# A fused attention and expert kernel: the expert's up products by one level of Strassen's scheme, with the weight sums loaded again for every pair of token chunks

## The chip, the core and the metric

The kernel runs on one core of a Trainium2 chip. The metric is the time of one execution on the device, in microseconds (us). The engines are named as in the profile: PE (TensorE, matrix products), PEld (PE's weight loads, listed apart), DVE (VectorE), ACT (ScalarE), POOL (GpSimd), SP (SyncE, which here only issues DMAs). PE reads its operands from the on-chip memory SBUF and writes to PSUM, which has 8 banks; a 128x512 tile of 32-bit numbers fills one bank.

## What is computed

```python
scores = scale * np.matmul(q, k.transpose(0, 1, 3, 2)) + bias   # 8 batches, 8 heads, 576 positions
attn = softmax(scores);  x = np.matmul(attn, v)                 # reshaped to 4608 tokens x 512

def _moe_ref(x, w1, w2, w3, w_out):      # 4608x512; 512x1024 twice; 1024x1024; 1024x512
    a = x @ w1
    b = x @ w2
    h = a * b @ w3
    return (h @ w_out).astype(np.float32)
```

The bias is a small network of the positions' distance. The expert weights come as 64-bit floats and are turned into 32-bit ones on the chip.

## The kernel before

The kernel has three stages. First it makes the bias; then it runs the attention of 32 units (pairs of heads by batches), whose result `x_d` (not yet divided by the softmax's sums) and the reciprocal sums `r_d` go to DRAM; then comes the expert. While attention still runs, the expert's weights `w3` and `w_out` are brought in, and `fold` multiplies them into one matrix (`folded`, L611), so that the expert is `(a * b) @ folded`.

Every 32-bit operand of a product is split into a high part in the reduced format fp32r and the rest: `xh` and `xl`, `wh` and `wl`, `gh` and `gl`. A product is three matmuls, high by high, low by high, high by low. So each split costs an ACT (or POOL) copy and a DVE subtraction.

The weights are turned into 32 bits by `narrow` (L121 to L150). Its steps for 512 columns are: one DMA (`wi`), two ACT instructions (L126, L129), four DVE instructions (L132, L135, L141, L146), and two POOL instructions (L149, L150), of which the first still reads `wi`. Before, `split_w` does this 16 times (8 blocks of 128 of the 1024 hidden columns, by `w1` and `w2`), then splits; all split weights stay in SBUF for the whole expert stage: the first two blocks in the pool `w01` on SBUF's right end, the other six in `wpool`.

The expert stage goes over 9 chunks of 512 tokens, and in each over the 8 blocks `ft`: 72 steps. In a step, `up` makes `a` and `b` for one block (24 matmuls of 128x512, L652), ACT copies `a` out of PSUM (L657), DVE multiplies it with `b` in PSUM (L660), and ACT and DVE split the product `g` (L663, L666); `down` multiplies the split product of the step before with `folded` (12 matmuls, L677), adding up over the 8 blocks in four PSUM banks `o`. `load_x` and `split_x` bring in and split the next chunk's tokens.

The order of the work on each engine is written out by hand: every piece of work is put into a list with a due time (`put(plan, steps, *times)`), and `drive` issues the pieces sorted by that time. An engine then takes its instructions strictly in that order, so one that waits holds up all behind it. The times are only used for sorting. `t_f` is the due time of the first expert step, and `end` that of attention's last piece. DMAs on SP are placed by the scheduler.

## Time and profile before

| what | value |
|---|---|
| median of 3 runs | 1249.78 us (1249.32 to 1249.95) |
| span of the profiled execution | 1248.1 us |
| PE busy | 1210.0 us (97%) |
| DVE, ACT, POOL busy | 653.6, 603.1 and 379.7 us |
| first matmul of the unbroken expert stage (`up`) | at 654.41 us |
| last group of matmuls (`o`) | from 1238.91 us, for 5.45 us |

The profiled execution's own span is 1248.1 us from the first to the last instruction, 1.7 us under the median of the runs; a change of the span is taken over to the median as it is. A matmul's listed duration holds its way through the pipeline; what one matmul costs in a row of them is the distance between starts, or the time of a group by its count.

### The profile page before, as it was taken

The page shows a single profiled execution, that of the slowest core. Times are in us where ns is not written, and L with a number is a line of the kernel's source. Part 1 is how long each engine was busy: PE and PEld are TensorE (multiplying, and loading weights), DVE is VectorE, ACT ScalarE, POOL GpSimd, SP SyncE. Part 2 cuts the span into 40 slices and gives each one's busy share as a digit, 9 for nine tenths or more (in the row PEclk, how much of TensorE's full clock was granted, in tenths as well). Part 3 has the DMA queues.
Part 4 walks back from the last instruction along what each step waited for, and adds up shares of the span by engine and source line. Part 5 has one row for each costly group of instructions (what it writes and reads, how often), then busy time and mean ns, then how long its engine had stood idle before and what let it go on. Part 6 is the DMA issues. An engine that isn't in the chain of part 4 may idle for free.

```text
span 1248.1 us, 19110 instructions
## 1 busy us (share of the span) xinstructions
PE 1210.0 (97%) x7200; PEld 964.2 (77%) x7200; DVE 653.6 (52%) x1380; ACT 603.1 (48%) x1295; POOL 379.7 (30%) x256
## 2 busy tenths in 40 slices
PE   6789999999999999999999999999999999999998
PEld 1368887777777788887678888888888888888887
DVE  8957776777677767775797522222212231313111
ACT  3768887888788878888444221212121212121211
POOL 5026664666466655661444300000000000000000
PEclk9989999999999999999999999999999999999999
DMA  4874446444644564521543121211111120200000
GB/s 149 285 234 144 142 147 202 142 142 141 222 123 151 151 219 134 145 81 54 133 147 110 60 68 34 68 34 51 51 51 51 42 61 34 68 34 1 20 15 34
DMA packets 60220, 130.26 MB, mean 104 GB/s; under 512 B 8928, under 2 KB 17504, under 8 KB 60128
## 3 DMA queue, kind: packets, MB, share of 16 engines
q1 hardware_dynamic: 59696, 129.02, 33.1%
q8 instruction: 57, 0.93, 0.3%
q14 instruction: 35, 0.29, 0.1%
q10 hardware_dynamic: 432, 0.02, 0.0%
HBM read 99.10 MB, written 29.92 MB: 103 GB/s over the span
## 4 chain that ended last, share of the span: by engine, by line
PE 81%; DVE 10%; DMA 4%; ACT 3%; issue 2%; SPq 0%; ACTq 0%; POOL 0%; DVEq 0%; POOLq 0%
PE up L652 32%; PE o L677 16%; PE pst L391 13%; PE s L284 11%; PE pst L349 5%; DVE r L322 4%; DVE ts L292 3%; PE wacc L611 2%; DMA nb_d<-bev 2%; ACT pt L357 2%; PE bacc L511 1%; DVE zdve L497 1%; DVE px L355 1%; DVE r L323 0%; DMA wi<-in_moe_w_dram 0%
## 5 line engine op out<-in xcount | busy, mean ns | idle before, releaser
L292 DVE CUSTOM_DVE_ANT_0 ts<-s,nb 128x576 f32<-128x576 f32 x256 | 184.6, 748 | 134.7 <-ACT pt L357 73.7
L660 DVE TENSOR_TENSOR g<-up,a 128x512 f32<-128x512 f32 x72 | 49.7, 691 | 343.4 <-PE up L652 343.4
L652 PE MATMUL up<-xh,wl 128*128 128x512 f32 x576 | 225.1, 391 | 0.0
L652 PE MATMUL up<-xl,wh 128*128 128x512 f32 x576 | 225.1, 391 | 0.0
L652 PE MATMUL up<-xh,wh 128*128 128x512 f32 x576 | 225.1, 391 | 0.0
L315 ACT ACTIVATE pp<-ts,mx 128x576 f32<-128x576 f32 x256 | 196.6, 769 | 42.5 <-DVE mx L292 42.5
L284 PE MATMUL s<-K,Q 128*128 128x288 f32 (+2 forms) x672 | 205.6, 325 | 9.2 <-ACT bev L518 3.7
L284 PE MATMUL s<-kl,Q 128*128 128x288 f32 (+2 forms) x672 | 182.3, 295 | 0.0
L677 PE MATMUL o<-w3s,gh 128*128 128x512 f32 x576 | 177.7, 390 | 0.0
L657 ACT COPY a<-up 128x512 f32<-128x512 f32 x72 | 42.2, 587 | 259.6 <-PE up L652 259.6
L638 POOL TENSOR_SCALAR xh<-xr 128x512 fp32r<-128x512 f32 x36 | 23.2, 646 | 445.4 <-DVE xr L634 442.7
L349 PE MATMUL pst<-ident,pp 128*128 128x128 f32 x1024 | 152.4, 277 | 0.2 <-ACT pt L357 0.2
L284 PEld LDWEIGHTS s<-K,Q 128*128 128x128 f32 x672 | 128.0, 191 | 30.1 <-DVE mx L292 13.6
L357 ACT ACTIVATE pt<-pst 128x512 f32<-128x512 f32 x224 | 129.4, 593 | 29.1 <-PE pst L349 24.8
L391 PE MATMUL pst<-pt,rv 128*64 128x320 f32 (+1 forms) x1024 | 138.3, 412 | 1.4 <-DVE pt L355 1.4
L663 ACT ACTIVATE gh<-g 128x512 fp32r<-128x512 f32 x72 | 45.5, 633 | 178.3 <-DVE g L660 178.3
L349 PEld LDWEIGHTS pst<-ident,pp 128*128 128x128 f32 x1024 | 118.5, 141 | 15.7 <-DVE wi L146 11.8
L284 PEld LDWEIGHTS s<-kl,Q 128*128 128x128 f32 x672 | 129.0, 192 | 0.0
L652 PEld LDWEIGHTS up<-xh,wl 128*128 128x128 f32 x576 | 108.2, 188 | 23.4
L652 PEld LDWEIGHTS up<-xl,wh 128*128 128x128 f32 x576 | 108.2, 188 | 23.4
L652 PEld LDWEIGHTS up<-xh,wh 128*128 128x128 f32 x576 | 108.2, 188 | 23.4
L677 PEld LDWEIGHTS o<-w3s,gh 128*128 128x128 f32 x576 | 108.1, 188 | 22.9
(87 smaller groups left out, 1734.2 us busy)
## 6 DMA issues: line engine op xcount, KB each, us to landing
rk<-in_k_dram SPq DMA_DIRECT2D x32, 576.0 KB
rq<-in_q_dram SPq DMA_DIRECT2D x32, 576.0 KB
wi<-in_moe_w_dram SPq DMA_DIRECT2D x32, 512.0 KB
nb_d<-bev SPq DMA_DIRECT2D x36, 295.5 KB
rv<-in_v_dram SPq DMA_DIRECT2D x32, 320.0 KB
x_d<-x SPq DMA_DIRECT2D x32, 288.0 KB
xr<-x_d SPq DMA_DIRECT2D x36, 256.0 KB
rb<-r_d SPq DMA_DIRECT2D x72, 128.0 KB
```

The source lines that it names most:

```text
L284: nc.tensor.matmul(o, l, r, start=(m == 0), stop=(m == len(ops) - 1))
L292: nc.vector.tensor_tensor_reduce(out=halves(ts), in0=d.pop(("s", t))[:, :, :HS], in1=halves(NB[p, t]), op0=ALU.add, op1=ALU.min, scale=-1. ...
L315: nc.scalar.activation(pp, ts, AF.Exp, bias=mx, scale=-1.0, accum_out=d["sum"][:, col:col + 1])
L322: nc.vector.tensor_scalar(r, d["sum"], 1e-9, None, op0=ALU.add)
L349: nc.tensor.transpose(ps[:, c * P:(c + 1) * P], x, ident)
L357: nc.scalar.activation(o, x, AF.Copy)
L391: nc.tensor.matmul(acc[rows], x[:, c0:c0 + D], m, start=(c == 0), stop=(c == 4))
L652: nc.tensor.matmul(acc, l[:, cc], r, start=(n == 0), stop=(n == 3 * NC - 1))
L657: nc.scalar.copy(a, ps[0])
L660: nc.vector.tensor_tensor(g, ps[1], a, op=ALU.mult)
L663: nc.scalar.activation(gh, g, AF.Copy)
L677: nc.tensor.matmul(d["o", t], l[:, sl], folded[ft][:, r], start=(ft == 0 and n == 0), stop=(ft == NF - 1 and n == 2),)
```

## The change

The expert works on 6 pairs of chunks of 384 tokens (called c and d) instead of 9 chunks of 512. For one block, `[a_c a_d; b_c b_d]` is a 2x2 block product: weights `[w1; w2]` cut in two halves of the inner dimension, tokens cut by chunk and by the same halves. Strassen's scheme (in Winograd's form) makes it with 7 block products instead of 8, from 4 more sums of weight blocks and 4 more sums of token blocks. A block product has 2 inner slices by 3 split terms, 6 matmuls of 128x384, so a step (pair, block) has 42 of them, and 18 matmuls of 128x512 in `down` (9 for d, 9 for c). There are 48 steps.

- `prep_w` replaces `split_w`: it runs `narrow` on both matrices of a block side by side, makes the 4 sums (L579), splits 7 blocks of weights (L583, L586) into one tile `wS` and writes it to DRAM (`w_d`, 1.83 MB for a block). Blocks 0 to 2 are prepared before the first step, blocks 3 to 7 in steps 0 to 4. `load_w` loads a block's `wS` again for each of pairs 1 to 5, into three buffers.
- `split_x` does the same for tokens: two multiplications of 768 columns (L654), 4 differences of 384 (L657), 7 copies and 7 subtractions (L663, L665), for each of two inner slices, once per pair.
- The 7 products accumulate in two PSUM banks `X` and `Y`: products 1, 6, 7, 4 in X, product 2 and then 5, 3 (called Z) in Y. Partial sums are read out between the products: by ACT (`p`, `u`, `z`; L705) and by DVE (`ac`, `bd`, `ad`, and the two products `gc`, `gd`; all L701). Each bank has one buffer, so the next product into a bank waits for the read before it. The other six banks hold the output sums.
- The buffers of `narrow` for the two matrices (pools `cva` and `cv2`) have one buffer each; before, `cv2` had two.

```diff
-    CH = 512
+    CH = 384
+    W2 = 2 * CH
-    STEP = 7.8
+    STEP = 11.40
-    cv = moe.enter_context(tc.tile_pool(name="cv2", bufs=2, side="right"))
+    cv = prep.enter_context(tc.tile_pool(name="cv2", bufs=1, side="right"))
+    bg = prep.enter_context(tc.tile_pool(name="bg", bufs=2, side="right"))
+    def prep_w(t):
+        big = bg.tile([P, 8, 2 * P], F32, name="big")
...
+            runs.append(narrow((cva, cv)[m], src, NC * P, flat[:, m * NC * P:(m + 1) * NC * P], nc.sync, pieces=NC))
+        for steps in zip(*runs):
+            for step in steps:
+                step()
+                yield
+        for o, x, y, op in ((4, 2, 3, ALU.add), (6, 0, 2, ALU.subtract), (5, 4, 0, ALU.subtract), (7, 1, 5, ALU.subtract)):
+            nc.vector.tensor_tensor(big[:, o], big[:, x], big[:, y], op=op)
+        yield
+        w = wr.tile([P, 2, 7, 2 * P], F32R, name="wS")
+        for o, x, n in ((0, 0, 2), (2, 3, 2), (4, 5, 2), (6, 7, 1)):
+            nc.scalar.activation(w[:, 0, o:o + n], big[:, x:x + n], AF.Copy)
+            yield
+            eng = nc.vector if o < 4 else nc.gpsimd
+            eng.tensor_tensor(w[:, 1, o:o + n], big[:, x:x + n], f(w[:, 0, o:o + n]), op=ALU.subtract)
+        nc.sync.dma_start(w_d[t], f(w.rearrange("p h s n -> p (h s n)")))
+        ups[0, t] = w
+    def load_w(p, t):
+        w = wr.tile([P, 2, 7, 2 * P], F32R, name="wS")
+        nc.sync.dma_start(f(w.rearrange("p h s n -> p (h s n)")), w_d[t])
...
+    AT_P = {"2": 0.0, "1": 1.04, "6": 4.2, "5": 5.25, "7": 6.3, "3": 7.3, "4": 10.4}
+    AT_E = {
+        "p": 2.10, "ac": 2.70, "u": 5.28, "z": 6.35, "bd": 7.32, "ad": 8.36, "gd": 8.95, "hd": 9.60, "ld": 10.15,
+        "gc": 11.45, "hc": 12.05, "lc": 12.60,
+    }
+    AT_D = {"d": 2.1, "c": 8.3}
+        if n in ("p", "u", "z"):
+            st[n] = temp("puz".index(n), n)
+            nc.scalar.copy(st[n], st["Z" if n == "z" else "X"])
+        elif n == "ac":
+            add("ac", 4, st["Y"], st["p"], ALU.add)
+        elif n == "bd":
+            add("bd", 3, st["X"], st["z"], ALU.add)
+        elif n == "ad":
+            add("ad", 5, st["Z"], st["u"], ALU.add)
+        elif n == "gc":
+            add("gc", 6, st["X"], st["ac"], ALU.mult)
+        elif n == "gd":
+            add("gd", 7, st["ad"], st["bd"], ALU.mult)
...
+    wr = moe.enter_context(tc.tile_pool(name="wr", bufs=3))
+    xs = moe.enter_context(tc.tile_pool(name="xs", bufs=1))
+    ps_ab = moe.enter_context(tc.tile_pool(name="ps_ab", bufs=1, space=PSUM))
```

How the rows move (in the rows of now, the lines from L579 on are the changed kernel's). First PE, in a late step of the expert stage. Before, a step begins with one block's 12 matmuls into `up0` and 12 into `up1` (here the last six into `up1`), and then the 12 of `down` into four output banks:

```order
L652 MATMUL up1_12187<-xh2_11656,wh17_8818 128x512
L652 MATMUL up1_12187<-xh2_11656,wl17_8820 128x512
L652 MATMUL up1_12187<-xl2_11657,wh17_8818 128x512
L652 MATMUL up1_12187<-xh3_11707,wh17_8818 128x512
L652 MATMUL up1_12187<-xh3_11707,wl17_8820 128x512
L652 MATMUL up1_12187<-xl3_11708,wh17_8818 128x512
L677 MATMUL o0_11922<-w3s6_8270,gh_12170 128x512 x2
L677 MATMUL o0_11922<-w3s6_8270,gl_12172 128x512
```

Now, from the start of the last step, products 2 and 1, the first output bank of d's `down`, and then products 6, 5 and 7 (each product is one row for each of the two inner slices):

```order
L692 MATMUL Y_13106<-xS0_12005,wS_12939 128x384 x3
L692 MATMUL Y_13106<-xS1_12301,wS_12939 128x384 x3
L692 MATMUL X_13117<-xS0_12005,wS_12939 128x384 x3
L692 MATMUL X_13117<-xS1_12301,wS_12939 128x384 x3
L732 MATMUL od0_12590<-w3s6_8283,ghd_13096 128x512 x2
L732 MATMUL od0_12590<-w3s6_8283,gld_13098 128x512
...
L692 MATMUL X_13117<-xS0_12005,wS_12939 128x384 x3
L692 MATMUL X_13117<-xS1_12301,wS_12939 128x384 x3
L692 MATMUL Y_13145<-xS0_12005,wS_12939 128x384 x3
L692 MATMUL Y_13145<-xS1_12301,wS_12939 128x384 x3
L692 MATMUL X_13117<-xS0_12005,wS_12939 128x384 x3
```

The matmuls are shorter and no longer alternate between spare banks: X_13117 is filled, read out and filled further within the step, and Y_13145 takes the bank of Y_13106.

Second ACT, among the expert's first steps. Before, in the first chunk, the copies `a` and `gh` of a step stand between the pieces of two blocks of `split_w` (`wmag`, `w` and `wh` belong to it):

```order
L126 ACTIVATE wmag<-wi 128x512
L129 ACTIVATE w<-wi 128x512
L657 COPY a<-up_8489 128x512
L568 ACTIVATE wh_8545<-w 128x512
L663 ACTIVATE gh<-g 128x512
```

Now, in step 1 of the first pair, from the two L126 of block 4's `prep_w` to the copies `p`, `u` and `z` (L705) of that step; the L583 rows belong to block 3:

```order
L126 ACTIVATE wmag<-wi 128x512 x2
L583 ACTIVATE wS<-big 128x512
L129 ACTIVATE big<-wi 128x512
L718 ACTIVATE ghc<-wos_8458 128x384
L129 ACTIVATE big<-wi 128x512
L583 ACTIVATE wS<-big 128x512 x2
L705 COPY wos_8494<-X 128x384
L583 ACTIVATE wS<-big 128x256
L705 COPY wos_8522<-X 128x384
L705 COPY wos_8530<-Y 128x384
```

Seven instructions of weight preparation and one split now stand ahead of `p` (`wos_8494`), the first of them behind a DMA.

Third DVE, at the same place. Before, `g` and `gl` of a step stand between the pieces of `split_w` and `split_x`:

```order
L132 TENSOR_SCALAR wmag<-wmag 128x512
L135 TENSOR_SCALAR wmag<-wmag 128x512
L660 TENSOR_TENSOR g<-up_8512,a 128x512
L141 SCALAR_TENSOR_TENSOR wmag<-wi,wmag 128x512
L571 TENSOR_TENSOR wl_8550<-w,wh_8545 128x512
L666 TENSOR_TENSOR gl<-g,gh 128x512
L146 TENSOR_SCALAR wi<-wmag 128x512
```

Now, in step 1 of the first pair, from the second L132 of block 4 to the sums of its weights, `ac` (`wos_8497`) stands ahead of the second half of `narrow`, and `bd`, `ad`, `gd` and the split `gld` behind it:

```order
L132 TENSOR_SCALAR wmag<-wmag 128x512
L135 TENSOR_SCALAR wmag<-wmag 128x512
L586 TENSOR_TENSOR wS<-big,wS 128x512
L135 TENSOR_SCALAR wmag<-wmag 128x512
L701 TENSOR_TENSOR wos_8497<-Y,wos_8494 128x384
L141 SCALAR_TENSOR_TENSOR wmag<-wi,wmag 128x512 x2
L146 TENSOR_SCALAR wi<-wmag 128x512 x2
L701 TENSOR_TENSOR wos_8545<-X,wos_8530 128x384
L701 TENSOR_TENSOR wos_8561<-Y,wos_8522 128x384
L701 TENSOR_TENSOR wos_8563<-wos_8561,wos_8545 128x384
L721 TENSOR_TENSOR gld<-wos_8563,ghd 128x384
L579 TENSOR_TENSOR big<-big 128x256 x4
```

So the weight preparation of a later block now waits for `ac`, which waits for `p` on ACT.

More of the change, by code (lines that the diff above doesn't have):

```diff
@@ L677, in down, with store, at, until @@
                 nc.tensor.matmul(
-                    d["o", t], l[:, sl], folded[ft][:, r],
+                    d["o", j, t], l[:, sl], folded[ft][:, r],
                     start=(ft == 0 and n == 0), stop=(ft == NF - 1 and n == 2),
                 )
-        yield
-        if ft == NF - 1:
-            for t in range(NT):
-                o = op.tile([P, DO], F32, name="osb")
-                nc.scalar.copy(o, d["o", t])
-                nc.sync.dma_start(out[c * CH + t * P:c * CH + (t + 1) * P, :], o)
-                yield
+    def store(p, j, t):
+        o = op.tile([P, DO], F32, name="osb")
+        move("DVE" if t == 1 else "ACT", (o, pairs[p]["o", j, t]))
+        r0 = p * W2 + "cd".index(j) * CH + t * P
+        nc.sync.dma_start(out[r0:r0 + P, :], o)
+    def at(time, step, *args):
+        later.append((time, len(later), lambda: step(*args)))
+    def until(time):
+        nonlocal later
+        now, later = [e for e in later if e[0] <= time], [e for e in later if e[0] > time]
+        drive(now)
     for i in range(NF):
```

199 lines of the change are left out of this document (107 added, 92 removed).

## The prediction

> **What bounds the kernel now.** I read the page first, then the chain of work that ended last, then the stretches of time around the start of the expert stage, and then the rows of single instructions. The chain in order of time (start, length, what) shows the expert stage as PE alone:
>
> ```profile
> span 1248.1 us, 19110 instructions
> 608.96 5.88 DMA wi<-in_moe_w_dram
> 648.83 5.58 PE wacc L611 x24
> 654.41 10.07 PE up L652 x43
> 1184.32 5.61 PE up L652 x24
> 1225.32 5.44 PE up L652 x24
> 1233.47 5.44 PE up L652 x24
> 1238.91 5.45 PE o L677 x24
> ```
>
> From 654.41 to 1238.91 + 5.45 = 1244.36 are 589.95 us, and a step starts every 8.15 us. So a matmul of 512 columns costs 5.44 / 24 = 0.2267 us. In the first two steps of a chunk, whose weights lie in `w01` at SBUF's right end, it costs 5.61 / 24 = 0.234, and in `fold`, whose weights lie on the right too, 5.58 / 24 = 0.2325. I call these the quick and the slow pace.
>
> Ahead of it, the stretches (length, then busy us and count of PE, PEld, DVE, ACT, POOL; clock, DMA share, GB/s) show DVE next to PE:
>
> ```profile
> 602.00:612.00 10.00, 8.75 (x44) 7.27 (x45) 8.18 (x14) 4.81 (x9) 2.65 (x2) 1.00 1.06 274
> 612.00:622.00 10.00, 9.02 (x45) 7.12 (x45) 5.48 (x11) 5.04 (x9) 3.65 (x4) 1.00 0.37 104
> 622.00:632.00 10.00, 7.97 (x30) 6.10 (x29) 9.50 (x14) 2.41 (x4) 4.94 (x6) 0.83 0.63 195
> 632.00:642.00 10.00, 10.00 (x52) 8.18 (x51) 8.63 (x12) 4.53 (x9) 5.66 (x4) 1.00 0.42 129
> 642.00:654.00 12.00, 12.00 (x59) 9.81 (x58) 11.52 (x18) 6.89 (x12) 5.63 (x4) 1.00 0.37 125
> ```
>
> In these 52 us DVE is busy for 43.3, and PE lost 4.3 us of the first 30. Anything that puts more on DVE here delays the expert's start.
>
> **The matmuls.** 384 columns occur nowhere; the nearest are the attention's scores of 288 columns, whose weights lie on the right:
>
> ```profile
> 400.42 0.29 PE L284 MATMUL s<-kl,Q 128*128 128x288 f32 x1
> 401.20 0.29 PE L284 MATMUL s<-kl,Q 128*128 128x288 f32 x1
> L284 PEld LDWEIGHTS s<-kl,Q 128*128 128x128 f32 x672 | 129.0, 192 | 0.0
> ```
>
> Six starts apart make 0.78 / 6 = 0.130 us for 288 columns; the slow pace has 0.2325 for 512. Both are 0.00045 us a column, so the cost goes with the columns. For 384 that gives 0.75 x 0.2267 = 0.170 at the quick pace and 0.75 x 0.2325 = 0.174 at the slow one. The new weights lie left, where the pace was quick; the token blocks of the odd pairs lie right, and whether that slows PE no row shows. I take 0.171, with 0.170 and 0.174 as ends. A step then costs 42 x 0.171 + 18 x 0.2267 = 7.18 + 4.08 = 11.26 us, 48 steps 540.6 us: **49.4 us gained** (42 to 51).
>
> The Trainium skill has a formula for this ("TensorE: Matmul & The Clock Gate", section Back-to-back issue gap): columns by 2.4 GHz and 2.5 ns on top. It would give 0.2158 for 512 columns, where this trace has 0.2267, and 0.1625 for 384; as an estimate from that page the gain would be 45 us and the sum 4 us higher. The measured pace stands.
>
> **The new evictions.** These are the rows by line and form (count, busy us, mean ns of one, idle before):
>
> ```profile
> L657 ACT COPY a<-up 128x512 f32<-128x512 f32 x72 | 42.2, 587 | 259.6 <-PE up L652 259.6
> L660 DVE TENSOR_TENSOR g<-up,a 128x512 f32<-128x512 f32 x72 | 49.7, 691 | 343.4 <-PE up L652 343.4
> L663 ACT ACTIVATE gh<-g 128x512 fp32r<-128x512 f32 x72 | 45.5, 633 | 178.3 <-DVE g L660 178.3
> L634 DVE TENSOR_TENSOR xr<-xr,rb 128x512 f32<-128x512 f32 x36 | 26.7, 743 | 0.0
> L605 DVE TENSOR_TENSOR w3l<-w3t,w3h 128x512 fp32r<-128x512 f32 x16 | 10.9, 682 | 4.1 <-ACT w3h L603 4.1
> L126 ACT ACTIVATE wmag<-wi 128x512 f32<-128x512 f32 x40 | 26.7, 667 | 7.1 <-DMA wi<-in_moe_w_dram 6.8 <-DVE w3l L605 0.3
> L129 ACT ACTIVATE w<-wi 128x512 f32<-128x512 uint32 x16 | 10.7, 670 | 0.0
> L132 DVE TENSOR_SCALAR wmag<-wmag 128x512 f32<-128x512 f32 x40 | 22.7, 568 | 3.9 <-ACT wmag L126 3.9
> L135 DVE TENSOR_SCALAR wmag<-wmag 128x512 int32<-128x512 int32 x40 | 20.8, 521 | 1.1
> L141 DVE SCALAR_TENSOR_TENSOR wmag<-wi,wmag 128x512 int32<-128x512 int32 x40 | 28.3, 707 | 0.2
> L146 DVE TENSOR_SCALAR wi<-wmag 128x512 int32<-128x512 int32 x40 | 18.0, 450 | 0.9
> L149 POOL TENSOR_TENSOR w<-w,wi 128x512 f32<-128x512 f32 x16 | 21.5, 1344 | 40.0 <-issue 20.2 <-ACT w L129 9.4 <-ACT wmag L126 5.5
> L150 POOL TENSOR_TENSOR w<-wmag,w 128x512 f32<-128x512 f32 x16 | 23.2, 1448 | 1.3
> ```
>
> Scaled to 384 columns, a read of PSUM costs 0.44 on ACT and 0.52 on DVE, a split 0.475 and 0.56. In a step of pairs 1 to 5, DVE has 7 of them (3.7 us) and ACT 5 (2.3 us) under 11.26 us of PE; the token splits add at most 4.5 us to a step. That is hidden as work. The waits are the question. Product 7 waits for `u`, product 3 for `z`, and the next step's product 1 for `gc`; each time, one product (6 x 0.171 = 1.03 us) covers the handover. Its legs, in four rows:
>
> ```profile
> 899.70 0.39 PE L652 MATMUL up<-xh,wl 128*128 128x512 f32 x1
> 899.73 0.59 ACT L657 COPY a<-up 128x512 f32<-128x512 f32 x1 [4.07 <-PE up L652]
> 616.62 0.69 DVE L605 TENSOR_TENSOR w3l<-w3t,w3h 128x512 fp32r<-128x512 f32 x1 [0.64 <-ACT w3h L603]
> 617.37 0.65 PE L599 MATMUL w3t<-ident,w3s 128*128 128x128 f32 x4 [0.98 <-DVE w3l L605]
> ```
>
> ACT starts 0.03 us after the next product's first matmul, and PE starts 0.06 us after DVE's end (617.31). So a handover takes 0.03 + 0.52 + 0.06 = 0.61 at most and has 0.4 us to spare: I cost these waits at nothing. The reload of `wS`, 1.83 MB a step, takes 6.7 us at the 274 GB/s of the first stretch above, and may start when the step three before ends, two steps (22 us) ahead: nothing as well. On SP it stands behind the loads of the next pair's tokens, which wait for the one `xr` and `rb` buffer, and at a pair's start behind the output stores, which wait for `down`'s last sums; both are ready within the step in which they stand, so the queue can hold a reload up by one step at most, of the two that it has. If that cover went, product 2 would be late next, by what is missing of 6.7 us. The stores themselves are as before, three at the end instead of four; I leave their half us out.
>
> **The start.** Between DVE's first `w3s` (601.9) and the fold's last `w3l` the new order has 14 `w3l` and 7 `w3s` (21 x 0.682 = 14.3), six rounds of `narrow` (6 x 2.246 = 13.5), 4 multiplications of 768 (4 x 1.11 = 4.5), 22 token differences and splits (22 x 0.56 = 12.3), 8 weight sums of 256 (8 x 0.37 = 3.0) and 4 weight splits (2.7): 50.3 us. With the 8.7 us of idle that the same stretch has now, it takes 59 instead of 52: **7 us lost**; nothing if the idle closes, 15 if the idle doubles.
>
> **The first pair.** Blocks 3 to 7 are prepared in steps 0 to 4. Each matrix has one `wi` buffer, so the second matrix of a block can be fetched only when POOL has read the last one, and its fetch stands ahead of `p` on ACT. The loop from landing to landing, in the order of the instructions: on ACT the second L126, a weight split, L129, `ghc`, L129, two weight splits and `p` (0.667 + 0.633 + 0.67 + 0.475 + 0.67 + 1.27 + 0.44 = 4.83); on DVE `ac`, two L141, one L146 (0.52 + 1.41 + 0.45 = 2.38); on POOL L149, L150, L149 (4.14); then the fetch:
>
> ```profile
> 684.40 0.37 SPq L121 DMA_DIRECT2D wi<-in_moe_w_dram  x1
> 687.93 0.67 ACT L126 ACTIVATE wmag<-wi 128x512 f32<-128x512 f32 x1 [0.73 <-DMA wi<-in_moe_w_dram]
> 670.74 1.62 POOL L150 TENSOR_TENSOR w<-wmag,w 128x512 f32<-128x512 f32 x1
> 671.14 1.51 DVE L132 TENSOR_SCALAR wmag<-wmag 128x512 f32<-128x512 f32 x1
> ```
>
> It takes 3.5 us here, and 5.88 in the chain above beside other transfers; beside the 1.83 MB store of `w_d` I take 4.3. With eight handovers of 0.05 the loop is 16.0 us, 4.8 more than a step of PE. Four loops lie between the five blocks: 19 us. In step 0 `p` comes 4.8 us after the landing instead of at product 1's end (2.1): 2.7. In step 3 one multiplication enters the loop: 1.1. In step 4 `gc` stands behind the four sums and a token split, and product 1 waits for it: about 3. Together **26 us lost**. The low end is DVE's bare work, 11.0 us a step and 8 more for the token blocks of steps 3 and 4: 8 us. The high end has the 5.88 us fetch and one blocking of DVE a loop, such as L132's 1.51 above, which ended with POOL's L150, against 0.568 on average: 19 us a loop, so 38 us. POOL is no bound here: 4 narrow instructions and two weight splits are some 7 us of the 16. PE will idle for 5 us a step; in the stretch from 622 to 632, with 2 us of idle, the granted clock fell to 0.83, and if it does so here the products get longer where PE waits anyway, so I add nothing.
>
> The Trainium skill gives a rule for that blocking ("SBUF — State Buffer", section SBUF: two separate sides): DVE and GpSimd share a port pair under an exclusive lock, and the loser waits for the whole instruction. The trace agrees (1.51 us). If it struck in each loop, the sum would be some 5 us higher.
>
> **The sum.** 1249.78 - 49.4 + 7 + 26 = 1233.4 us. The sum is made in the profiled span, 1.7 us under the median, and carried over.
>
> **Rivals.**
> - *The bank handovers miss* (slower). If `u`, `z` and `gc` each come x us late, that is 3 x 48 x = 144 x: 0.13 us each over their slack cancels what the sum has left, 0.2 gives about 1262. For it: with one bank each, every product waits for a read. Against it: the slack of 0.4 us. Chance 0.12.
> - *Weight loads set the pace* (slower). A load lasts 0.192, more than 0.171. If loads went one behind the other, a step would be 42 x 0.192 + 4.08 = 12.14 us, the gain only 7 us, and the time 1276. Against it: the scores run at 0.130 with loads of 0.192. Chance 0.03.
> - *The first pair is hidden after all*: both losses at their low ends, 1249.8 - 49.4 + 2 + 10 = 1212. For it: a fetch of 3.5 us and POOL shorter than its listed spans. Chance 0.15.
> - *Gain and losses cancel*, at their high ends: about 1250. Chance 0.10.
> - My forecast, 1222 to 1246, has the remaining 0.60.
>
> The range from 1211 to 1256 leaves out some 2 in 10. A change of 0.2% (2.5 us) is about what this measurement can tell: faster 0.73, the same 0.10, slower 0.17.
>
> **What would show it.** Pairs 1 to 5: 11.2 to 11.4 us a step, PE without idle time; if idle time stands before L692 there, the first rival holds. Steps 0 to 4: about 16 us each, PE idle behind ACT's `p` and DVE's `gc`, ACT's L126 behind DMA `wi`. First product 2 some 7 us after 654. I am wrong if the steps of the later pairs are above 11.7 us, or if those of the first pair are not above 12.

## The result: the kernel is 0.6% slower

The changed kernel takes 1258.2 us (1256.9 to 1259.3 in four runs) against 1249.9 in the same comparison: a ratio of 1.0061, interval 1.0047 to 1.0076. The forecast was 1233.5. First the page of the changed kernel, its span and the busy times of the engines:

```profile
span 1256.4 us, 20346 instructions
PE 1185.7 (94%) x7488; PEld 998.4 (79%) x7488; DVE 796.5 (63%) x1700; ACT 669.3 (53%) x1479; POOL 378.9 (30%) x236
```

PE works 24 us less than before and yet the span is 8.3 us longer. The stretches of time say where PE stands idle (length, then busy us and count of PE, PEld, DVE, ACT, POOL; clock, DMA share, GB/s):

```profile
632.00:642.00 10.00, 7.20 (x35) 5.69 (x35) 6.70 (x14) 1.79 (x3) 5.08 (x4) 1.00 0.87 306
664.00:700.00 36.00, 27.08 (x121) 24.28 (x120) 25.57 (x49) 15.36 (x31) 16.32 (x13) 0.88 0.55 197
700.00:750.00 50.00, 38.10 (x170) 32.23 (x169) 44.43 (x71) 20.28 (x42) 25.74 (x18) 0.92 0.46 168
800.00:1200.00 400.00, 400.00 (x2086) 373.24 (x2086) 195.81 (x355) 118.12 (x246) 0.00 (x0) 1.00 0.57 205
```

From 800 to 1200 PE is never idle. Between 664 and 750 it lacks 20.8 us, DVE is the busiest engine beside it (44.4 of the last 50), and the granted clock is 0.88 and 0.92. The matmuls into bank Y show when steps begin. In step 0 product 1 was done ahead, inside the fold, so its rows into Y are products 2, 5 and 3; then come the first products 2 of step 1 (678.84), of steps 6 and 7, and of two late steps:

```profile
665.66 1.21 PE L692 MATMUL Y<-xS,wS 128*128 128x384 f32 x6
672.11 2.29 PE L692 MATMUL Y<-xS,wS 128*128 128x384 f32 x6 [3.00 <-DVE wos L701]
678.84 1.21 PE L692 MATMUL Y<-xS,wS 128*128 128x384 f32 x6
763.91 1.20 PE L692 MATMUL Y<-xS,wS 128*128 128x384 f32 x6
775.40 1.20 PE L692 MATMUL Y<-xS,wS 128*128 128x384 f32 x6
1224.21 1.22 PE L692 MATMUL Y<-xS,wS 128*128 128x384 f32 x6
1235.73 1.22 PE L692 MATMUL Y<-xS,wS 128*128 128x384 f32 x6
```

An undisturbed step takes 11.49 us where the tokens lie on the left (763.91 to 775.40) and 11.52 where they lie on the right. Steps 0 to 5 would take 6 x 11.49 less product 1 and less `down`, which step 0 has not: 63.7 us. They took 763.91 - 665.66 = 98.25, so the first pair lost 34.6 us.

Not all of that is idle time. PE stands idle for 22.6 of the 98.25 us; in the other 75.7 it does what takes 63.7 undisturbed. Most of that difference is the granted clock, which was 0.50 in four stretches, at about 671 to 677, 698 to 701, 729 to 735 and 753 to 756 us. Two pieces of them, and product 7 of step 0, which lies in the first:

```profile
672.00:677.00 5.00, 4.89 (x15) 4.89 (x16) 2.49 (x6) 0.48 (x1) 3.25 (x3) 0.50 0.90 356
730.00:735.00 5.00, 5.00 (x15) 4.50 (x16) 4.28 (x11) 3.79 (x8) 0.00 (x0) 0.50 0.51 127
674.20 2.12 PE L692 MATMUL X<-xS,wS 128*128 128x384 f32 x6
```

Product 5 took 674.20 - 672.11 = 2.09 us there, where an undisturbed product takes 1.04. By the distances between starts, the longer matmuls of the four stretches add up to 8.8 us; the last 3.2 go mostly to the ends and the first matmuls of PE's runs, at some twelve stops. Each of the four stretches came with or shortly after an idle time of PE of 2.4 to 5.0 us, while one of 2.5 us (before product 1 of step 1) brought none, so no limit is read from this.

The last group of attention's products shows when the expert's start could begin, in the chain of before and in that of after:

```profile
595.43 2.84 PE pst L391 x20
```

```profile
597.63 2.84 PE pst L391 x20
```

From its end to the first product 2 of the expert (before, the first `up`) are 654.41 - 598.27 = 56.1 us before and 665.66 - 600.47 = 65.2 now. I call this the start's distance. Attention itself ended 2.2 us later, though its work is unchanged. In the ten kernels below with the same attention this group starts at 595.9 to 599.0 (the last in e1, whose expert has no Strassen products), so I take the 2.2 us as the difference of one execution from another.

| part | forecast | measured |
|---|---|---|
| expert matmuls, undisturbed | -49.4 | -38.8 |
| start's distance | +7 | +9.1 |
| end of attention in this execution | - | +2.2 |
| first pair | +26 | +34.6 |
| from the last step to the end (by what is left) | -0.5, left out | +1.3 |
| sum | -16.4 | +8.4 (span: +8.3) |

The -38.8 is 763.91 to 1247.25 for steps 6 to 47, plus 63.7 and the last `down` of 4.1, against 589.95; 1.0 of it is product 1 of step 0, done ahead in the fold. So the forecast failed by two terms above all: the matmuls gained 10.6 us less, and the first pair lost 8.6 us more.

### The profile page after: what moved, and what is told of

Same layout as the page of the kernel before. It is cut to its first block, busy times and chain, and to the rows that moved or that the text cites. A ratio compares the mean times of both kernels' runs of the same rounds, so it can differ in the third digit from the quotient of the medians.

```text
span 1256.4 us, 20346 instructions
## 1 busy us (share of the span) xinstructions
PE 1185.7 (94%) x7488; PEld 998.4 (79%) x7488; DVE 796.5 (63%) x1700; ACT 669.3 (53%) x1479; POOL 378.9 (30%) x236
## 4 chain that ended last, share of the span: by engine, by line
PE 72%; DVE 15%; DMA 4%; ACT 4%; issue 2%; POOL 2%; SPq 0%; ACTq 0%; DVEq 0%; POOLq 0%
PE X L692 15%; PE pst L391 13%; PE Y L692 11%; PE s L284 11%; PE od L732 7%; PE oc L732 7%; PE pst L349 5%; DVE r L322 4%; DVE ts L292 3%; ACT pt L357 2%; DMA nb_d<-bev 1%; PE bacc L511 1%; DVE xS L665 1%; DVE zdve L497 1%; POOL big L149 1%
## 5 line engine op out<-in xcount | busy, mean ns | idle before, releaser
L292 DVE CUSTOM_DVE_ANT_0 ts<-s,nb 128x576 f32<-128x576 f32 x256 | 184.6, 748 | 135.4 <-ACT pt L357 74.1
L692 PE MATMUL X<-xS,wS 128*128 128x384 f32 x1152 | 237.4, 341 | 18.1 <-DVE wos L701 16.6
L692 PEld LDWEIGHTS X<-xS,wS 128*128 128x128 f32 x1152 | 207.3, 190 | 29.6 <-DVE wos L701 19.2
L692 PE MATMUL Y<-xS,wS 128*128 128x384 f32 x864 | 177.4, 340 | 4.5 <-DVE wos L701 4.5
L692 PEld LDWEIGHTS Y<-xS,wS 128*128 128x128 f32 x864 | 155.6, 191 | 5.9 <-DVE wos L701 5.8
L701 DVE TENSOR_TENSOR wos<-X,wos 128x384 f32<-128x384 f32 x96 | 53.4, 557 | 151.0 <-PE X L692 151.0
L349 PEld LDWEIGHTS pst<-ident,pp 128*128 128x128 f32 x1024 | 118.6, 141 | 15.7 <-DVE wi L146 11.8
L705 ACT COPY wos<-X 128x384 f32<-128x384 f32 x96 | 45.9, 478 | 137.7 <-PE X L692 137.6
L391 PEld LDWEIGHTS pst<-pt,rv 128*64 128x64 f32 x1024 | 67.8, 136 | 50.1 <-issue 10.4
L732 PE MATMUL od<-w3s,ghd 128*128 128x512 f32 x288 | 91.9, 401 | 0.0
L732 PE MATMUL oc<-w3s,ghc 128*128 128x512 f32 x288 | 89.6, 392 | 0.0
L701 DVE TENSOR_TENSOR wos<-Y,wos 128x384 f32<-128x384 f32 x96 | 53.4, 556 | 54.1 <-ACT wos L705 37.9
L251 POOL TENSOR_TENSOR Q<-rq,Q 64x1152 fp32r<-64x1152 f32 x32 | 85.4, 2669 | 2.7
```

The lines of the kernel that those rows point to most:

```text
L251: nc.gpsimd.tensor_tensor(Qd[hi], x[hi], f(Qd[hi]), op=ALU.subtract)
L292: nc.vector.tensor_tensor_reduce(out=halves(ts), in0=d.pop(("s", t))[:, :, :HS], in1=halves(NB[p, t]), op0=ALU.add, op1=ALU.min, scale=-1. ...
L349: nc.tensor.transpose(ps[:, c * P:(c + 1) * P], x, ident)
L391: nc.tensor.matmul(acc[rows], x[:, c0:c0 + D], m, start=(c == 0), stop=(c == 4))
L692: nc.tensor.matmul(acc, w[:, l, W_AT[n], i * P:(i + 1) * P], x[:, r, X_AT[n]], start=(k in "125" and i == 0 and m == 0), stop=(i == 1 and ...
L701: nc.vector.tensor_tensor(st[o], x, y, op=op)
```

## The experiments

A ratio is that of a kernel's times to those of before, run on the same chip; the changed kernel's own is 1.0061.

| kernel | median us | ratio (interval) | start's distance | first pair lost |
|---|---|---|---|---|
| changed kernel | 1258.2 | 1.0061 (1.0047 to 1.0076) | 65.2 | 34.6 |
| e3, no preparation of blocks 3 to 7 | 1225.1 | 0.978 (0.9758 to 0.9802) | 64.6 | 1.9 (8 steps) |
| e4, second raw-token buffer | 1257.3 | 1.0037 (1.002 to 1.0054) | 63.6 | 35.1 |
| e5, two `wi` buffers | 1271.4 | 1.0176 (1.0154 to 1.0198) | 64.9 | 30.5 |
| e6, preparation spread | 1246.3 | 0.9965 (0.995 to 0.9979) | 66.5 | 22.8 (8 steps) |
| e7, spread and later | 1252.8 | 1.0014 (1.0 to 1.0028) | 65.3 | 30.3 (8 steps) |
| e9, e7 with e4 | 1249.7 | 0.9999 (0.9983 to 1.0015) | 63.8 | 30.5 (8 steps) |
| e10, no token split in the first pair | 1254.0 | 1.0017 (1.0002 to 1.0033) | 64.7 | 31.6 |
| e11, blocks 4 to 7 converted in attention | 1236.7 | 0.988 (0.986 to 0.9901) | 63.8 | 13.0 |
| e12, all blocks | 1271.3 | 1.0161 (1.0137 to 1.0186) | 59.4 | 5.0 |
| e13, e12 with a new start | 1264.9 | 1.01 (1.0079 to 1.0121) | 51.5 | 6.1 |
| e14, e11 with a new start | 1233.9 | 0.9863 (0.9841 to 0.9884) | 61.9 | 12.0 |
| e15, e14 with blocks 3 to 6 | 1235.2 | 0.9873 (0.9849 to 0.9898) | 61.9 | 14.1 |
| e16, POOL's part of narrow on DVE | 1257.2 | 1.0044 (1.003 to 1.0059) | 64.5 | 33.9 |
| e17, e14 with that | 1234.0 | 0.986 (0.9844 to 0.9877) | 62.7 | 11.0 |

One correction to the expectations below: in those of e3 to e7 and e9 I took the row at 672.11 for the first product 2. It is product 5 of step 0; product 2 stands at 665.66. So "28 us" of the first pair there is 34.6, "6.5 us forward" in e7's text was no change at all, and the "8 us" that the second buffer is said to bring in those of e7 and e9 is 1.6. The waits of DVE for tokens that the texts of e4 and e14 give as 8.3, or 6 and 8 us, were 3.3, or 3.0 and 3.3 (see e4).

### What a matmul of 384 columns costs (e1, e2)

```diff
-    CH = 512
+    CH = 384        # e2: 256; both in the kernel before
```

> The kernel before, with chunks of 384 tokens instead of 512 (12 chunks, the same plain 24 up matmuls a step, no Strassen). It measures the pitch of a 384-column matmul by itself. Theory A (a matmul has a fixed cost: 512 columns cost 0.2267 us = 512 / 2.4 GHz + 13.4 ns, so 384 cost 0.160 + 0.0133 = 0.1733 us): 24 matmuls take 4.16 us in the steps with weights on the left. Theory B (the prediction's: the cost goes with the columns, and the 0.1733 to 0.1746 us of the changed kernel come from its own pattern, six matmuls into one bank and then a change of bank): 24 matmuls take 4.08 us here (0.170 each). For the first two blocks of a chunk, whose weights lie on SBUF's right end, A says 0.180 each (4.32 us), B 0.1755 (4.21 us).

> The kernel before, with chunks of 256 tokens (18 chunks): a third point for the pitch. Theory A (fixed cost of 13.4 ns a matmul): 0.1067 + 0.0134 = 0.120 us each, 24 in 2.88 us. Theory B (cost goes with the columns): 0.1133 us each, 2.72 us. If something else than PE sets the step here (evictions of 72 steps become 144), the pitch is read within a block of 12 matmuls.

The chain of e1 in the expert stage (start, length, what), and a row of e2's:

```profile
802.58 4.18 PE up L652 x24
808.84 4.16 PE up L652 x24
815.08 4.17 PE up L652 x24
```

```profile
785.14 2.87 PE up L652 x24
```

A matmul of 384 columns costs 4.18 / 24 = 0.1742 us and one of 256 costs 0.1196, beside 0.2267 for 512. Theory A holds for weights on the left, and the plain kernel without any Strassen products has the same price. Between 256 and 512 a column costs (0.2267 - 0.1196) / 256 = 0.418 ns; 256 columns at that price are 0.107, so 0.0126 us of every matmul do not depend on its columns. The steps at 808.84 and 815.08, whose weights lie on SBUF's right end, are not slower: the slow pace that both theories priced at 0.1755 to 0.18 did not show at 384 columns. (The kernels took 1267.6 and 1284.6 us in their one run, as shorter chunks need more matmuls.)

### The weight preparation (e3, e10)

```diff
-    for t in range(NF):              # e3: which blocks prep_w makes
+    for t in range(3):
-        w, n = ups[p, t], int(k)
+        w, n = ups[p, t % 3 if p == 0 else t], int(k)
```

> The changed kernel without the weight preparation of blocks 3 to 7: in the first pair their products use the weights of blocks 0 to 2, and the later pairs load those three again from DRAM (the same bytes). The number of matmuls, evictions, token splits and loads stays. Theory A (the preparation in steps 0 to 4 costs the first pair its 28 us): the first six steps take 11.5 us each but for the token splits, the loss falls from 28 to 2 to 6 us, and the kernel takes 1232 to 1237 us. Theory B (the handovers between the two banks or the token splits of the second pair, which stand in steps 3 to 7, hold the first pair): at least 15 of the 28 us stay, and the kernel takes 1245 us or more.

Product 2 of step 0 and of step 8 in e3:

```profile
665.65 1.22 PE L692 MATMUL Y<-xS,wS 128*128 128x384 f32 x6
754.24 1.21 PE L692 MATMUL Y<-xS,wS 128*128 128x384 f32 x6
```

Eight undisturbed steps are 86.7 us here; these took 88.6, and the granted clock stayed at 1.00. That is theory A; its time came out 7 us too high since it reckoned with 28 us instead of 34.6. So 32.7 of the 34.6 us come with the preparation of blocks 3 to 7, 6.5 us a block, and the span fell by just that, from 1256.4 to 1223.8. The bank handovers and the token splits by themselves cost the first pair 1.9 us at most. The start is where it was: block 3's preparation does not delay it.

```diff
     def split_x(p, i):               # e10
+        if p == 1:
+            ...
+            nc.sync.dma_start(f(x), f(pairs[0]["x"][i]))
+            return
```

> The changed kernel without the token split of the second pair, which stood in steps 3 to 7 of the first: the second pair uses a copy of the first pair's split tokens, brought by a DMA. The weight preparation stays as it is. The first pair lost 34.5 us against undisturbed steps (product 2 of step 0 at 665.66, step 6 at 763.91), and 1.9 without the preparation of blocks 3 to 7 but with the token split. Theory A (each costs its own: the weight loop of 16 us a block alone): at least 28 us stay lost, 1253 us or more. Theory B (the two meet on DVE, whose bare work of 82 us in the first pair nearly fills PE's 87, so the split costs 10 to 15 us where the preparation runs, though 2 alone): 20 to 25 us lost, 1245 to 1251 us.

It lost 31.6 us, as theory A said, though a little of that is its own: the copies slowed one fetch to 8.47 us. What it shows best is the loop. ACT's L126 of the second matrix of blocks 4 to 7 (start, length, idle time before it):

```profile
685.30 0.67 ACT L126 ACTIVATE wmag<-wi 128x512 f32<-128x512 f32 x1 [0.77 <-DMA wi<-in_moe_w_dram]
700.66 0.67 ACT L126 ACTIVATE wmag<-wi 128x512 f32<-128x512 f32 x1 [0.93 <-DMA wi<-in_moe_w_dram]
716.41 0.67 ACT L126 ACTIVATE wmag<-wi 128x512 f32<-128x512 f32 x1 [1.32 <-DMA wi<-in_moe_w_dram]
732.30 0.66 ACT L126 ACTIVATE wmag<-wi 128x512 f32<-128x512 f32 x1 [1.07 <-DMA wi<-in_moe_w_dram]
```

The distances are 15.4, 15.8 and 15.9 us; the forecast had 16.0. In the changed kernel itself, blocks 3 to 6:

```profile
668.66 0.65 ACT L126 ACTIVATE wmag<-wi 128x512 f32<-128x512 f32 x1
681.03 0.67 ACT L126 ACTIVATE wmag<-wi 128x512 f32<-128x512 f32 x1 [0.47 <-DMA wi<-in_moe_w_dram]
697.72 0.67 ACT L126 ACTIVATE wmag<-wi 128x512 f32<-128x512 f32 x1 [0.93 <-DMA wi<-in_moe_w_dram]
713.04 0.66 ACT L126 ACTIVATE wmag<-wi 128x512 f32<-128x512 f32 x1 [0.86 <-DMA wi<-in_moe_w_dram]
731.33 1.25 ACT L126 ACTIVATE wmag<-wi 128x512 f32<-128x512 f32 x2
```

Here they are 12.4, 16.7, 15.3 and 18.9 (the last row holds both matrices of block 7), and only the last, into which the token split of steps 3 and 4 falls, does not wait for the DMA.

### The loop, or the work in it? (e5, e6, e16)

```diff
-            wi = pool.tile([P, n, 2], I32, name="wi")
+            wi = (raw or pool.tile)([P, n, 2], I32, name="wi")   # e5: raw alternates between two buffers
-    op = moe.enter_context(tc.tile_pool(name="op", bufs=NT))
+    op = moe.enter_context(tc.tile_pool(name="op", bufs=2))      # makes room for them
```

> The changed kernel with two buffers for the raw weights (wi) of each matrix instead of one, so that a block's weights can be fetched while the block before is still being converted. The first pair lost 28 us against undisturbed steps; without the preparation of blocks 3 to 7 it lost 2. Theory A (the prediction's: a loop from landing to landing, which the one buffer closes and in which the fetch of 3 to 4.5 us and POOL's two operations stand): the steps of the first pair fall from 17 us to 13 to 14, the kernel takes 8 to 14 us less than the changed one, 1245 to 1251 us. Theory B (the engines' orders: p, ac and gc stand behind the preparation's instructions on ACT and DVE, whenever the weights land): less than 3 us gained, 1255 us or more.

```profile
679.38 1.21 ACT L126 ACTIVATE wmag<-wi 128x512 f32<-128x512 f32 x2
693.23 1.23 ACT L126 ACTIVATE wmag<-wi 128x512 f32<-128x512 f32 x2
706.20 1.23 ACT L126 ACTIVATE wmag<-wi 128x512 f32<-128x512 f32 x2
727.18 1.25 ACT L126 ACTIVATE wmag<-wi 128x512 f32<-128x512 f32 x2
```

The fetch no longer holds ACT up, and blocks 4 to 6 follow each other in 13.9 and 13.0 us. But the next distance is 21.0: that is where the token split stands in the orders, and step 3 still took 20.5 us instead of 21.8. PE reached the steps after the first pair 4 us earlier than in the changed kernel, not 8 to 14 (theory A) and not under 3 (theory B). The total of 1271 says nothing on this, since the missing output buffer cost more at the ends of later pairs: from 800 to 1200 PE was busy for 392.25 us instead of 400. So the one buffer does close the loop, but opening it gave the first pair only 4 us.

```diff
-        t0 = end + 4.5 + 14.0 * t if t < 3 else t_f - 1.0 + STEP * (t - 3)
+        t0 = end + 4.5 + 14.0 * t if t < 3 else t_f - 1.0 + 1.3 * STEP * (t - 3)
```

> The changed kernel with the preparation of blocks 3 to 7 spread over more steps: a block every 1.3 steps (14.8 us) instead of every step (11.4 us); block 3 begins where it did. Same work, other places in the orders. Theory A (a loop of some 16 us a block): a block's loop exceeds its 14.8 us of PE's steps by 1 to 2 us instead of 5, so the first pair's loss falls from 28 to 10 to 16 us, and the kernel takes 1245 to 1251 us. Theory B (the amount of work is what counts, wherever it stands, and each block holds PE up for its 5 us): 1255 us or more.

Theory A: 1246.3 us, 12 us of the first pair regained by one number, and faster than before by 0.35% (interval 0.2 to 0.5%). That the same work meets fewer other instructions in each step is my reading of it; e7 below, nearly as far spread, regained only 4 us.

```diff
-            nc.gpsimd.tensor_tensor(x, x, f(d["power"]), op=ALU.mult)
-            nc.gpsimd.tensor_tensor(x, d["mag"], x, op=ALU.add)
+            eng.tensor_tensor(x, x, f(d["power"]), op=ALU.mult)   # e16: eng is nc.vector for blocks 3 to 7
+            eng.tensor_tensor(x, d["mag"], x, op=ALU.add)
```

> The changed kernel with the last two operations of narrow (L149 and L150) for blocks 3 to 7 on DVE instead of POOL. This gives DVE 20 more instructions of some 0.6 us (12 us) in the first pair. Theory A (POOL's instructions stretch DVE's: 15 us of DVE's 82 busy us in the first pair, and the loop of a block has 4.1 us of POOL in it): the loop becomes 2 us shorter, DVE is no fuller than before, and the kernel takes 4 to 10 us less, 1248 to 1254 us. Theory B (DVE's own instructions fill it, and the stretching lies beside waits anyway): 12 us more on DVE make the first pair longer, 1261 us or more.

The result, 1257.2, lies between the two theories. Groups of DVE's instructions from 665.6 to 764 (count, busy us, mean ns), first in the changed kernel, then in e16:

```profile
L146 DVE TENSOR_SCALAR wi<-wmag 128x512 int32<-128x512 int32 x10 | 6.1, 631 | 0.0
L665 DVE TENSOR_TENSOR xS<-xr,xS 128x384 fp32r<-128x384 f32 x7 | 6.0, 867 | 0.0
L657 DVE TENSOR_TENSOR xr<-xr 128x384 f32<-128x384 f32 x4 | 5.3, 1352 | 0.0
L701 DVE TENSOR_TENSOR wos<-X,wos 128x384 f32<-128x384 f32 x11 | 6.1, 552 | 8.7 <-PE X L692 8.7
L701 DVE TENSOR_TENSOR wos<-wos,wos 128x384 f32<-128x384 f32 x6 | 5.0, 834 | 0.2
```

```profile
L149 DVE TENSOR_TENSOR big<-big,wi 128x512 f32<-128x512 f32 x10 | 6.8, 681 | 0.0
L146 DVE TENSOR_SCALAR wi<-wmag 128x512 int32<-128x512 int32 x10 | 3.9, 415 | 0.0
L665 DVE TENSOR_TENSOR xS<-xr,xS 128x384 fp32r<-128x384 f32 x7 | 4.3, 627 | 0.0
L657 DVE TENSOR_TENSOR xr<-xr 128x384 f32<-128x384 f32 x4 | 2.0, 552 | 0.0
L701 DVE TENSOR_TENSOR wos<-wos,wos 128x384 f32<-128x384 f32 x6 | 3.4, 559 | 0.2
```

In the changed kernel one of the four L657 met no instruction of POOL and took 557 ns, the three beside POOL's took 1609 to 1633; in e16, where none met one, all four took 549 to 558. In the same way L665, L146 and L701 of two SBUF tiles were stretched, together by 3.2 + 1.7 + 2.2 + 1.6 = 8.7 us. L701 with a PSUM bank as one operand was not (552 ns, and 554 in e16). e16 took these 9 us off DVE and put some 14 us on it, 6.8 of L149 and as much of L150, and its span is 1.7 us shorter, 1254.7. That both count, a full DVE and POOL's stretching in it, is my reading; e16 also took POOL's 4.1 us out of the loop, and the ratios' intervals overlap, so all that is shown is that the exchange changed next to nothing. The Trainium skill has the rule for this ("SBUF — State Buffer", section Who interferes with whom): a DVE instruction with two SBUF inputs contends with a GpSimd instruction that reads SBUF; one with at most one SBUF input doesn't, except in certain modes that the section allows for `tensor_scalar` among others. The `L701` rows and L657 agree. L146 and L135, each a TENSOR_SCALAR that reads one SBUF tile, were stretched too (from some 415 ns up to 1511 and 1512), and whether they ran in such a mode no run here shows.

### Later, or with another buffer (e4, e7, e9)

```diff
-        xr = xs.tile([P, 8, CH], F32, name="xr")
+        xr = (xt[0] if (p, i) == (0, 1) else xs).tile([P, 8, CH], F32, name="xr")   # e4
```

> The changed kernel with a second buffer for the raw tokens of the first pair, so that the second inner slice's tokens can be fetched while the first slice is still being split. Theory A (at the start DVE waits for that fetch, 8.3 us from 632.89 to 641.18): the first product 2 comes 6 to 9 us earlier than 672.1, and the kernel takes 1249 to 1252 us. Theory B (the start is bound by DVE's work and by POOL's sums, the fetch only stands beside them): it comes less than 2 us earlier, 1256 to 1258 us.

The chain of the changed kernel holds two fetches of tokens at the start, of 5.77 us (from 605.96) and 8.27 us (from 632.89). DVE works on during most of both; its own waits for them are the numbers at the end of these rows:

```profile
610.44 0.96 DVE L654 TENSOR_TENSOR xr<-xr,rb 128x768 f32<-128x768 f32 x1 [2.97 <-DMA rb<-r_d]
641.18 1.25 DVE L654 TENSOR_TENSOR xr<-xr,rb 128x768 f32<-128x768 f32 x1 [3.30 <-DMA xr<-x_d]
```

So theory A had at most 3.3 us to win. e4 takes that wait away, and its product 2 comes at 664.05, 1.6 us earlier: theory B. DVE's stretches there are now full:

```profile
632.00:642.00 10.00, 9.33 (x47) 7.78 (x48) 10.00 (x18) 3.18 (x6) 5.15 (x3) 1.00 0.71 249
642.00:654.00 12.00, 9.44 (x39) 7.42 (x38) 11.96 (x20) 7.54 (x16) 4.86 (x4) 0.86 0.76 222
```

```diff
+        t0 = end + 4.5 + 14.0 * t if t < 3 else t_f + 3.0 + 1.25 * STEP * (t - 3)   # e7; e9 adds e4's buffer
```

> Like the spread kernel (a block every 1.25 steps), and the preparation of block 3 is placed 4 us later, so that its first half stands behind the start of the expert stage. Leaving the preparation out altogether had brought the first product 2 forward by 6.5 us. Theory A (block 3's preparation delays the last token splits and fold pieces on DVE, ACT and POOL): product 2 comes 3 to 6 us earlier than 672.1, and the kernel takes 1240 to 1248 us, 3 to 6 less than the spread one. Theory B (what starts earlier is waited for again in the first pair, as with the second raw-token buffer, where 8 us at the start became 3 at the end): within 2 us of the spread kernel.

> Like the kernel with block 3 later and a block every 1.25 steps, with the second raw-token buffer for the first pair besides. In the changed kernel that buffer alone brought product 2 forward by 8 us and the end by 3, since the weight preparation then held the first pair. Theory A (with the preparation spread, the first pair has room, and what is won at the start stays): product 2 at 658 to 662, 6 to 9 us less than the kernel without the buffer, 1232 to 1240 us. Theory B (the preparation still holds the first pair): less than 4 us less than that kernel.

The start's distance of e7 is the same as the changed kernel's (65.3), so placing block 3 later brought it nothing, and the first pair lost 7.5 us more than in e6; its step 6 still took 15.1 us, where e6's took 11.8. Neither theory held: it took 6.5 us more than the spread kernel. That the later blocks then meet the token splits is my reading of it, and was not tested by itself. e9's buffer brought 1.5 us of distance again, and 3 us of the time: theory B.

### Taking the conversion out of the stage (e11 to e15, e17)

Attention runs one conversion of `w3` or `w_out` in each of 24 of its 32 units. e11 gives the other 8 units the `narrow` of blocks 4 to 7:

```diff
+    n_d = {t: dram.tile([P, 2 * NC * P], F32, name=f"n_d{t}") for t in range(4, NF)}
+    def early(t, m):                 # narrow into a buffer, then a store to n_d[t]
+    for j, u in enumerate([u for u in range(NU) if u not in pieces]):
+        pieces[u] = early(4 + j // 2, j % 2)
...
+        if t in n_d:                 # in prep_w, in place of the two runs of narrow
+            nc.sync.dma_start(flat[:, 0:2 * NC * P], n_d[t])
```

> The changed kernel with the conversion to 32 bits of blocks 4 to 7 (8 of the 16 runs of narrow) moved into those 8 attention units that had none, with a store to DRAM and a load in the first pair; sums and splits stay where they were. Theory A (the conversions' loop of ACT, DVE, POOL and fetch holds the first pair up; attention, with DVE 73% busy, can take 8 conversions for 1 us each at most): the first pair loses 6 to 12 us instead of 34.5, the kernel takes 1228 to 1238 us. Theory B (the sums, the splits and the wait of a block's first product for them are what counts): 20 us or more stay lost, 1245 us or more. Theory C (attention pays: each of the 8 units becomes 2 us or more longer): the end of attention comes 16 us later, 1245 to 1255 us.

```profile
664.00:700.00 36.00, 29.21 (x132) 25.82 (x131) 21.75 (x42) 13.18 (x27) 12.82 (x12) 0.91 0.47 169
700.00:750.00 50.00, 48.94 (x254) 44.84 (x253) 35.18 (x64) 18.97 (x40) 7.21 (x7) 1.00 0.66 237
```

From 700 to 750 DVE fell from 44.4 to 35.2 busy us and PE stands for 1 us. The first pair lost 13.0 instead of 34.6: 21.6 us for 4 blocks, 5.4 each. The time of 1236.7 is in the range of theory A (its loss just outside the 6 to 12) and beats the kernel before by 1.2%.

e12 moves blocks 0 to 3 as well, as a second conversion in 8 units; e13 adds e4's buffer and other due times for the first pair's token splits.

```diff
+    for j in range(8):               # e12
+        put(later, run(early(j // 2, j % 2, Spare())), *((1.5 + 3 * j) * PERIOD + o for o in offs))
...
-        t0 = end + 6.0 + 19.0 * i    # e13 and e14
-        put(later, split_x(0, i), t0 - 4.0, ...
+        t0 = end + (10.0, 23.0)[i]
+        put(later, split_x(0, i), end + (2.0, 12.0)[i], ...
```

> The kernel with early conversion, for all 8 blocks: the conversions of blocks 0 to 3 now also run in attention, as a second piece of work in 8 of its units, in buffers of w3's late blocks that are still empty there. With blocks 4 to 7 alone the time was 0.988 of before (1236.7 us); the first pair then still lost 13 us (product 2 of step 0 at 666.81, step 6 at 743.51, against 63.7 undisturbed) and the start 12. Theory A (conversion work on DVE, ACT and POOL holds the start and steps 0 and 1): 13.5 us of DVE work leave the start and 4.5 step 0, product 2 comes 5 to 10 us earlier, the first pair loses 5 to 8, the kernel takes 1219 to 1229 us. Theory B (the token splits, the fold and the fetch of the tokens hold the start): product 2 comes less than 3 us earlier, 1230 us or more. Theory C (attention pays for a second conversion in a unit, with DVE at 80%): 1236 us or more.

> Like the kernel with all conversions in attention, with the second raw-token buffer for the first pair, and the first slice's multiplications and splits due 4 us later in the orders (DVE waited 6 us for its tokens at the start of the fold, with other work behind that wait). Theory A (DVE's idle time in these two waits, some 9 us, is what is left of the start's loss): product 2 another 5 to 9 us earlier, 1213 to 1223 us. Theory B (DVE has nothing else ready to do while it waits, or the fold's own pace on PE, ACT and DVE sets the start): within 2 us of the other.

Attention's last group of products in e12:

```profile
634.22 2.84 PE pst L391 x20
```

It comes 34.0 us later than in e11, 4.3 us for each of the eight second conversions: theory C. From 100 to 590 us PE waits 21.5 us for the results `mx` of DVE's L292, in e11 0.6. These two kernels vary by more than others (e12 from 1259.9 to 1274.9; this is the trace of its fastest run). Yet behind attention both other theories are answered. Without any conversion the first pair lost 5.0 us and step 0 nothing, and the start's distance fell to 59.4, 4.4 us under e11's; DVE then waited 9.2 us for tokens. With these waits gone as well (e13) it fell by another 7.9, to 51.5, less than the kernel before had. In e4, which takes the longer of the token waits away, and e14, which leaves DVE none, conversions stay in the start, and the distance fell by 1.6 and 1.9. So the start is made of conversion work and token waits, and each hides the other as long as both are there.

e14 is e11 with e13's start, e15 the same with blocks 3 to 6 in attention:

> The kernel with the conversion of blocks 4 to 7 in attention (0.988 of before; product 2 of step 0 at 666.8), with the second raw-token buffer for the first pair, and the first slice's multiplications and splits due 4 us later, the second slice's 2 us earlier, on DVE and ACT. Theory A (DVE's two waits for tokens, 6 and 8 us, with other work queued behind them, set the start): product 2 comes 5 to 9 us earlier, 1228 to 1233 us. Theory B (DVE's work and POOL's chain for block 2 set it, as the buffer alone suggested, which brought 1.6 us): less than 3 us earlier, 1234 us or more.

> As the one before, but blocks 3 to 6 are converted in attention instead of 4 to 7; block 7 is converted in steps 4 and 5. Theory A (block 3's conversion, whose L126, L132 and L135 stand ahead of p and ac, holds steps 0 and 1, which lost 6 and 4.5 us): these two lose less than 4 us together, and the kernel takes 4 to 8 us less than the one before. Theory B (the splits of block 2 and the token splits hold step 0; block 7's conversion then costs as much later): within 3 us of the one before.

e14's product 2 comes at 664.08, 2.7 us earlier than e11's (666.81), and the time is 1233.9: theory B. Product 2 of steps 0, 1 and 2 in e15, then in e14:

```profile
662.69 1.20 PE L716 MATMUL Y<-xS,wS 128*128 128x384 f32 x6
669.57 1.22 PE L716 MATMUL Y<-xS,wS 128*128 128x384 f32 x6
685.20 1.21 PE L716 MATMUL Y<-xS,wS 128*128 128x384 f32 x6
```

```profile
664.08 1.22 PE L716 MATMUL Y<-xS,wS 128*128 128x384 f32 x6
677.40 1.20 PE L716 MATMUL Y<-xS,wS 128*128 128x384 f32 x6
691.43 1.21 PE L716 MATMUL Y<-xS,wS 128*128 128x384 f32 x6
```

Undisturbed, step 0 takes 6.3 us. It takes 6.9 without block 3's conversion and 13.3 with it: that is what held `ac`, and with it product 5 (the 3.00 us before 672.11 above). Steps 0 and 1 still lose 4.7 us together, not under 4. The time stays the same, as block 7's conversion then costs steps 4 and 5 as much: theory B by its time, while step 0 itself went as theory A said. e14 is, at 1233.9 us, with e17 the fastest version: 1.4% under before.

> The fastest version so far (blocks 4 to 7 converted in attention, second raw-token buffer, the first slice's splits later; 0.9863 of before, 1233.9 us) with the same two operations of blocks 0 to 3 on DVE instead of POOL, so 16 more instructions of DVE in the start and step 0. Theory A (POOL's instructions stretch DVE's by 9 us in the start of that version): product 2 comes 1 to 4 us earlier than 664.1, step 0 loses less than its 6 us, 1228 to 1232 us. Theory B (10 us more on a full DVE): product 2 later by 2 us or more, 1236 us or more.

Neither theory: nothing changed (0.986 against 0.9863), as in e16.

## Why the prediction was wrong

- **"The cost goes with the columns": wrong, and with the first pair the largest miss.** It rested on two quotients that agreed, the scores' 0.130 us for 288 columns and the slow pace's 0.2325 for 512. But the slow pace holds some 6 ns that 384 columns do not show, and so the agreement was chance: by e1 and e2 each matmul has some 13 ns that do not shrink. At 0.1742 instead of 0.171 the 42 products of a step take 7.32 us instead of 7.18; the rest of the 11.51 us is `down` at about 0.230 instead of 0.2267, and a slower first product after it. So of the 10.6 us some 6.5 come from this step of the prediction (42 x 0.0032 x 48), the rest mostly from `down`, which was carried over at its old price. The later steps, 11.49 to 11.52 us, lie above the 11.2 to 11.4 forecast and under the 11.7 that I had named as the sign of being wrong. The Trainium skill's formula in the prediction ("TensorE: Matmul & The Clock Gate", section Back-to-back issue gap) has the right form, a price by columns and a fixed one; its fixed 2.5 ns are too few here, and its gain of 45 us was also too high, but nearer to the 38.8 than my 49.4. The prediction leaves out that the section gives it for a matmul by itself; for a stream with weight loads it names about 131 ns at 512 columns, where this case measured 226.7.
- **Bank handovers, the reload of `wS`, SP's queue: right.** PE is busy for 400.00 of 400 us from 800 to 1200, where all of them happen. The two slow rivals are refuted, weight loads at 0.19 us included.
- **The start, 7 us: 9.1, near.** The forecast had 50.3 us of DVE work and 8.7 of idle. From 602.00 to product 2 at 665.66 DVE was busy for 48.4 us and idle for 15.3, of which 6.3 behind tokens, 4.7 behind ACT's pieces of the fold and 3.8 behind POOL. So the nearness is in part luck: less work than reckoned, more waiting.
- **The granted clock, "so I add nothing": a term put at nothing, wrong for about half of it.** The prediction saw the clock fall to 0.83 beside 2 us of idle, and put the longer matmuls at nothing because they would come where PE waits anyway. In the first pair the clock was 0.50 in four stretches, and their matmuls took 8.8 us more, of which 2.6 in step 0. PE's idle time itself was 22.6 us, not more than the 26 forecast. In the second stretch PE waited for `ac` behind it anyway, as assumed. But in and behind the first and the last, 2.6 and 1.7 us of the 8.8, DVE stood waiting for PE's products (2.50 and 1.01 us from 674 to 678, 5.41 us up to 759.99), so there the slow matmuls were themselves what held the step. How much of the 8.8 us a full clock would have given back no run shows by itself; e3 and e12, the kernels that lose least, ran at 1.00 from 700 to 750.
- **The first pair, 26 us: right in its loop, too small in its sum.** The loop of 16.0 us is there: 15.4 to 15.9 in e10, and four distances in the changed kernel that exceed four steps by 17.3 us, where 19 were forecast. Mis-sized was what lies around it. Step 0 lost 6.9 us (678.84 - 665.66 - 6.3) instead of 2.7: 1.1 behind `p`, 3.3 behind `ac`, 2.6 by the clock. I had counted block 3's instructions ahead of `p` but not those ahead of `ac` on DVE. Step 3 lost 10.3; there the second pair's token split stands on a DVE that POOL stretches (L657 at 1352 ns), and I had priced the split at its bare work. Without the split (e10) that step lost 4.7. The stretching was in the prediction as a rule that would add 5 us if it struck in each loop; it struck, by 9 us or more of DVE time, but e16 does not show what PE paid for it.
- **The rival "gain and losses cancel"**, with 0.10, was nearest. What I did not do was to add up DVE's work for the whole first pair. The bare 11.0 us a step that the prediction itself gave, beside 11.26 of PE, say that no wait of DVE's there could be hidden. Smaller slips change nothing: this rival's own high ends (15 and 38) make 1253 and not about 1250, the low ends of the rival before it (nothing and 8) make 1208 and not 1212, and L132's 1.51 us ended 0.3 us after POOL's L150 and not with it.

What stays open: how much of the loss around the loop is the token split's, and how much the clock's. e10 puts the split at 3 us, or up to 4 more if its slow fetch is allowed for.

## What to carry to other kernels

A matmul has a price that does not depend on its columns, so a scheme that saves products by shorter matmuls saves less than the count of columns says; measure the pitch at the new width in the plain kernel first. A stage in which an engine's own work nearly fills PE's time has no cover for any wait: spread that work over more steps (12 us here by one number, but only 4 with another placing) or move it to a stage with room, one piece for each place that is still free (some 20 us), and not a second piece where a place is taken (34 us lost). Where PE will stand idle for some us at a time, look at the granted clock in the profile before pricing the matmuls that follow at full speed. When the removal of a wait brings nothing, look for what filled its place before calling the wait harmless, and read the engine's own idle time, not the length of the transfer that the chain shows.
